# A two-part block on one core: the second 256-token feed-forward block takes the seven-product form, the first one is written out as single jobs, and keys x values and numerators go in eleven chunks of three heads

## The chip, the core and the metric

One Trainium2 chip, one of its cores. The metric is the device time of one execution in microseconds (us). The kernel before was run three times apart from its profile: 374.29, 374.99 and 375.0 us, median 374.99. One more execution was profiled: 374.21 us, in which the program's own span is 372.4 us.

## What is computed

```python
sa, ca, ga, sb, cb, gb = split(silu(c) @ w_mod)          # six rows of 576
h = layernorm(x) * (1 + ca) + sa                          # x: 2048 x 576
q, k, v = split(h @ wqkv)                                 # 32 heads of 18
phi(t) = concat(softmax(t @ w_phi), softmax(-(t @ w_phi)))   # 36 features a head, q and k
kv, z = phi(k)^T v, sum(phi(k))                           # linear attention, a head at a time
x = x + ga * ((phi(q) kv / (phi(q) z + 1e-6)) @ wo)
h = layernorm(x) * (1 + cb) + sb
x = x + gb * (relu(h @ w1) @ w2)                          # w1: 576 x 4608, w2: 4608 x 576
```

All inputs and the output are bf16.

## The kernel before, in words

**Tiles and stages.** The 2048 tokens are 16 tiles of 128. The kernel has three stages.

1. *Setup and the walk over the tokens.* The weights of k and q are folded with w_phi on TensorE (jobs `FK`, `FQ`), three rows of constants are added to the folded weights so that the layernorm's mean and shift come out of the same product (jobs `KR`, `VR`, `QR`), and for each tile the products K, V and Q are made (`proj`, ten matmuls of 116 rows x 288 columns each). ScalarE takes the exponentials, VectorE the sums, GpSimd the ratios. `kv` (line 331) adds each tile's phi(k)^T v into two PSUM banks.
2. *Attention and feed-forward, in eight blocks of two tiles.* For a block, `num_mm` (line 401) makes the numerators and denominators, `num_o` divides, a DMA transposes, `wo_mm`/`project` (lines 418, 958, 965) or seven products (lines 984, 989) make the output projection; then the second layernorm; then layer 1 (h @ w1, relu) and layer 2 (the product with w2, in seven products of 18 matmuls of 288 columns, line 890).
3. *The end*: the last half product, its sum and the stores.

**Layer 1 has two forms.** Blocks 0 and 1 use `l1` (line 744): 324 matmuls of 64 rows x 128 columns of weights, each with 256 tokens moving (324 is 18 pairs of column blocks x 9 chunks of 64 features x 2; two matmuls with different halves of the 128 rows run beside each other). Blocks 2 to 7 use `l1_seven` (lines 793 and 810): 7 products of half size in place of 8 (Strassen's scheme), in 512 matmuls with 128 tokens moving and 36 with 256. The seven products need sums of the weights (`w1_sum`, line 486, 512 or 2048 elements a partition at a time, in place, once) from additional copies of w1 parts (`w1_more`), and sums of the features of each block (`t_feat`, line 868, four a block). The constant `BS = 2` is the number of blocks in the old form.

**Keys x values in nine chunks.** phi(k) of a tile is 1152 columns wide (32 heads x 36). Before, these are cut into nine pieces of 128, which don't fall on the heads' borders: a piece touches four or five heads, so `kv` has nine matmuls a tile with 76 columns (five of them) or 95 (four), and a mask takes out what belongs to other heads. `num_mm` uses the same nine pieces, one split at a bank's border: ten matmuls a tile with 76 (four), 95 (four) and 38 columns (two).

**What sets the order of the work.** `tc.manual_schedule()`: each engine runs its instructions in the order in which the program issues them. For stage 1, and for stage 2 up to the first layernorm of the feed-forward, that order is the string `ORDER`, one word a job (`K7:1` is the K product of tile 7 into PSUM pair 1; `eK7` its exponentials on ScalarE; `sK7` the sums on VectorE; `pM7` a GpSimd job; `LwqT` a load on the SyncE queue). Blocks 0 and 1 are then driven by hooks called between the matmuls (`b0_l1`, `in_l1`, `in_l2`), blocks 2 to 7 by the string `SEVEN` and hooks. All loads, stores, transposes and round trips through DRAM are issued on one queue, SyncE's (SP); one load is on ScalarE's.

**What the steps of the prediction touch.** `spin` (line 238) are matmuls on zeros that fill TensorE's time at the start. `rows_mm` (line 276) makes the K and V constant rows with ten matmuls of 288 columns; the Q row goes through `quarters` (line 373), twenty matmuls of 144 columns with 32 columns of weights, of which four run beside each other. `add_res` (line 426) adds a projection to x and so frees the two PSUM banks that it read; `relu` (lines 752 to 754) has two ScalarE instructions and one on VectorE; `t_part` (line 512) makes sums of w2; `q_sm` (lines 292 and 350) sums a tile of phi(q); `ln2_apply` (line 435) applies the second layernorm.

Of the kernel before, what the change touches and what calls it, by code (L numbers as in the profile page):

```python
# [7 lines left out]
P = 128  # L8
# [24 lines left out]
KVC = [((P * c) // E36, (P * c + P - 1) // E36) for c in range(9)]  # L33
# [3 lines left out]
for _c, (_a, _b) in enumerate(KVC):  # L37
    _k = 0 if _c < 5 else 1
    KVO.append((_k, _o[_k]))
    _o[_k] += (_b - _a + 1) * VW  # L40
# [8 lines left out]
Lt2 pM1 V1:0 m2:2 eK3 FQ0:3 Lx6 vE0 V2:1 Lwga vE1 rK2 Lx10 m2c FQrd0 pA2 FQ1:3 xa4 sp4 Lt4 bn7 vE2 T4:2 Tc4 K4:0 FQra1  # L49
eK4 FQ2:2 xp6 bn6 sa6 FQrd2 sK3 Lt3 bn11 K5:1 pM2 kv0 kv1 QR:2 eK5 V3:0 kv2 QRh sp6 QRe QRd T6:2 rK3 sK4 pA3 vE3 rp  # L50
Tc6 pM3 K7:1 rK4 K6:2 pM4 pA4 eK7 eK6 Lwgb ga:0 gac V4:1 bn9 kv3 sK5 rK5 bn8 pA5 w2b0 sa8 V5:2 vE4 bn12 sp8 T8:0 xa8
pM5 vE5 Tc8 Q0:1 eQ0 gb:2 xp14 kv4 kv5 sK6 bn10 Q1:0 gbc sa10 sK7 gaw gar wl1 rK6 K8:1 qs0 wl3 bn15 eQ1 eK8 K9:2 eK9
sp10 xp10 Lwo Q2:0 pA6 sK8 pM6 eQ2 V6:1 rK8 bn13 vE6 sK9 bn14 qp0 rK7 Q3:2 pA8 T10:0 Tc10 pA7 eQ3 qs1 pM7 kv6 K10:1
eK10 rK9 K11:0 sK10 pM8 V8:2 eK11 sa14 sa12 V7:1 vE8 pM9 rK10 V9:0 vE7 xa12 sp12 pA9 kv7 T12:2 sK11 rK11 kv8 V10:1 vE9
kv9 wl0 pA10 vE10 Tc12 pM10 K12:0 sp14 T14:2 Tc14 gbw eK12 kv10 K13:1 eK13 wo2 K14:2 eK14 qt0 qs2 sK12 sK13 Q4:0 eQ4
rK13 K15:1 w2a1 qp1 V11:2 V12:0 gbr qs3 wo1 pA11 qp2 pM11 vE11 kv11 w2a2 rK12 w2a0 pA12 eK15 vE12 sK15 pM12 qt1 V13:2
kv12 pM13 Lmask sK14 Q5:1 wl4 rK15 eQ5 sq5 Q6:0 pA13 pA15 vE13 sq4 kv13 qt2 V15:2 rK14 vE15 pM15 pA14 V14:1 vE14 eQ6
Q11:2 pM14 qp3 sq6 kv14 kv15 qt3 eQ11 sq11 Q7:1 kz nu1:2 Q8:0 nu0:3 nO1 td2 eQ7 eQ8 sq7 nO0 td0 sq8 ot1:2 td1 Q9:1 oc1
Q10:0 ot0:2 wo0 wo4 eQ9 qi5 wo3 sq9 oc0 eQ10 W1:3 xr1 qi4 W0:1 lb1 Q12:2 xr0 lb0 Q13:0 lr1 eQ12 sq10 qi6 lr0 ap1 eQ13
Q14:1 ht1:2 Q15:3 ap0 wl2 ht0:0 ha eQ14 eQ15 hd w2b1 sq13 sq15 sq14 sq12  # L60
# [16 lines left out]
BS = 2  # L77
# [4 lines left out]
def tile_block(ctx, tc, a, out):  # L82
# [18 lines left out]
    x_sb = small([P, NT, D], BF16, "x_sb")  # L101
# [3 lines left out]
    NEQ, NE, NV, NL = 6, 5, 4, 3  # L105
    TW = 18 * HD
    RTL = 17920
    RT = small([P, RTL + NL * 2 * D], BF16, "RT")
    v_sb = carve(RT, 0, (NV, H * VW))
    E_sb = carve(RT, NV * H * VW, (NE, 2 * D))  # L110
    xT_hi = NE * 2 * D + NV * H * VW
    EQ = carve(RT, xT_hi + 8 * NC * P, (NEQ, 2 * D))
    SLOT = (0, 1, 2, 3, 4, 5, 0, 1, 2, 3, 4, 5, 0, 1, 2, 3)
    EL = carve(RT, RTL, (NL, 2 * D))
    eqd = dram.tile([P, NT, 2 * D], BF16, name="eqd")
    NET = 4
# [28 lines left out]
    kvz = small([P, KVW], BF16, "kvz")
    ga_row = small([P, D], BF16, "ga_row")
# [84 lines left out]
    pool.memset(epsz, 0.5e-6)  # L231
    pool.memset(m98[:], 0.0)
# [40 lines left out]
    def rows_mm(raw, pr):  # L273
        for k in range(2):
            for ck in range(NC):
                pe.matmul(pr[0:NX, k, 0:HD], lhsT=m98[0:R, ck, :], rhs=raw[0:R, ck, k * HD:(k + 1) * HD],
                          start=(ck == 0), stop=(ck == NC - 1))

# [6 lines left out]
    def exps(t, pr, E):  # L285
        for s in range(2):
            act.activation(out=E.rearrange("p (b h s e) -> p b h s e", b=2, s=2, e=DH)[:, :, :, s, :],  # L287
                           in_=pr[:, :, 0:HD].rearrange("p b (h e) -> p b h e", e=DH),
                           func=ACT.Exp, scale=rs[:, t, s:s + 1])

    def sums(E, Rr):
        dve.tensor_reduce(out=Rr, in_=E.rearrange("p (c e) -> p c e", e=DH), axis=AXX, op=ALU.add)

# [33 lines left out]
    def kv(t):  # L327
        E = E_sb[:, t % NE, :]
        for c in range(9):
            k, o, n = kvcols(c)  # L330
            pe.matmul(PS[:, 6 + k, o:o + n], lhsT=E[:, c * P:(c + 1) * P],  # L331
                      rhs=v_sb[:, (t + 1) % NV, KVC[c][0] * VW:KVC[c][0] * VW + n],
                      start=(t == 0 and o == 0), stop=(t == NT - 1), skip_group_check=True)
# [4 lines left out]

    def eq(u):
        return EQ[:, SLOT[u], :] if u < QF else EL[:, u % NL, :]  # L340

    def q_out(u):
        sp.dma_start(eqd[:, u, :], EQ[:, SLOT[u], :])

    def q_in(u):
        sp.dma_start(EL[:, u % NL, :], eqd[:, u, :])

    def q_sm(u):
        sums(eq(u), Rq[:, u % 2, :])
        dve.reciprocal(out=rq[:, u % 2, :], in_=hs(Rq[:, u % 2, :], 1))  # L350

    def q_pool(u):
        pool.tensor_tensor(out=ratq[:, u % 2, :], in0=hs(Rq[:, u % 2, :], 0), in1=rq[:, u % 2, :], op=ALU.mult)
        minus(pool, eq(u), ratq[:, u % 2, :])

    def eslot(u):
        return u % NET if u < 8 else u % 2

    def q_turn(u):
        sp.dma_start_transpose(ET[:, eslot(u)], eq(u).rearrange("p (c f) -> p c f", f=P))  # L360
# [21 lines left out]
    def row_r(k):  # L382
        sp.dma_start((ga_row, gb_row)[k][:], gatd[k:k + 1].rearrange("a g f -> a (g f)").to_broadcast([P, D]))

    def num_mm(t, pr):
        seen = set()
        parts = []
        for c in range(9):
# [5 lines left out]
        for i, (c, h0, h1) in enumerate(parts):  # L394
# [6 lines left out]
            pe.matmul(pr[:, k, b:b + n], lhsT=ET[:, eslot(t), c, :], rhs=kvz[:, o:o + n],  # L401
# [60 lines left out]
    w21 = x_sb[:, 8:16, :].rearrange("p a b -> p (a b)")[:, 0:4096]  # L462
# [29 lines left out]
    TF = carve(RE.bitcast(FP16), 2 * 9 * P, (4, 4, P))  # L492
# [32 lines left out]

    def rows_h(pr, k):
        c = slice(k * HD, (k + 1) * HD)
        act.activation(out=tmpr[X0:NX, c], in_=pr[X0:NX, k, 0:HD], func=ACT.Copy)

    def rows_d(pr, dst, k):  # L530

        c = slice(k * HD, (k + 1) * HD)
        dve.scalar_tensor_tensor(out=dst[X0:NX, 4, c], in0=tmpr[X0:NX, c], scalar=mk[X0:NX, :],
                                 in1=pr[X0:NX, k, 0:HD], op0=ALU.mult, op1=ALU.add)
# [20 lines left out]
    def scale():  # L555
        dve.tensor_scalar(out=ca1[0:R, :], in0=PS[0:R, 7, 0:NC], scalar1=1.0, scalar2=None, op0=ALU.add)
        dve.tensor_scalar(out=m98[0:R, :, X0:X0 + 3], in0=ca1[0:R, :].unsqueeze(2).to_broadcast([R, NC, 3]), scalar1=-1.0,
                          scalar2=None, op0=ALU.mult)

    def x_scale(t, eng):  # L560
# [6 lines left out]
        for ck in range(NC):  # L567
# [64 lines left out]

    def t_cols(t, pr):
        for j in range(2):
            pe.transpose(bf(pr[:, 0, :])[:, j * P:(j + 1) * P], sc[:, (t + j) % 4, :], ident[:, 0:P])

    def rows_copy(t, pr):
        act.activation(out=xt_rows(t, 2), in_=bf(pr[:, 0, :])[X0:NX, 0:2 * P], func=ACT.Copy)  # L638

    def stats_a(t):  # L640
        act.activation(out=lnv[:, t:t + 2], in_=mv[:, 0, t:t + 2, 1], func=ACT.Ln, bias=eps_t[:], scale=1.0)
        act.activation(out=rs[:, t:t + 2, 0], in_=lnv[:, t:t + 2], func=ACT.Exp, scale=-0.5)
        act.activation(out=sc[:, t % 4:t % 4 + 2, X0 + 3], in_=lnv[:, t:t + 2], func=ACT.Exp, scale=0.5)

    def stats_p(t):
        c = sc[:, t % 4:t % 4 + 2, :]
        pool.tensor_copy(c[:, :, X0:X0 + 2], mv[:, 0, t:t + 2, 0:1].to_broadcast([P, 2, 2]))
        pool.tensor_tensor(out=c[:, :, X0 + 2], in0=mv[:, 0, t:t + 2, 0], in1=c[:, :, X0], op=ALU.subtract)
        pool.tensor_scalar(out=rs[:, t:t + 2, 1], in0=rs[:, t:t + 2, 0], scalar1=-1.0, scalar2=None, op0=ALU.mult)

    def k_scale(t):
        pool.tensor_scalar(out=Ak[:, t % 4, :], in0=hs(rk[:, t % 4, :], 0), scalar1=rs[:, t, 0:1], scalar2=None, op0=ALU.mult)

    def k_minus(t):
        Rr, r = Rk[:, t % 4, :], rk[:, t % 4, :]
# [646 lines left out]
```

## Time and profile before

| | |
|---|---|
| median of three runs | 374.99 us (374.29 to 375.0) |
| the profiled execution, its own time | 374.21 us |
| its span | 372.4 us |
| TensorE (PE) busy | 365.9 us of the span |
| VectorE (DVE) busy | 291.5 us |
| ScalarE (ACT) busy | 225.3 us |
| GpSimd (POOL) busy | 147.3 us |
| granted TensorE clock | 1.0 |
| PE waits that the trace names, all | 2.5 us, all before 18 us |

How it is read: an engine's busy share over the span says little by itself, since stages have different limits; what counts is the chain of work that ended last, which the profile follows back from the last instruction, and the order on each engine's queue. The duration of one matmul in a group's row is from issue to its end, with much of it overlapped by the next: the spacing of the starts is what a matmul costs TensorE.

### The profile page before, as it was taken

The numbers are of one execution on the slowest core, as the hardware profiler recorded it, in microseconds if no ns is written. First come the engines' busy times: TensorE is split into PE (matmuls) and PEld (weight loads), VectorE is DVE, ScalarE is ACT, GpSimd is POOL, SyncE is SP. The second block draws the span as 40 slices with busy tenths as digits, with TensorE's granted clock in tenths as the row PEclk, the third lists the DMA queues.
The fourth block names the chain that finished last, engine by engine and source line by source line (L and its number), as shares of the span: only waits on it lengthen the run. The fifth ranks groups of instructions, "written<-read, shape, count | busy, mean of one in ns | idle before, by whom it ended". The sixth has DMA issues, their size and how long they took to land.

```text
span 372.4 us, 14350 instructions
## 1 busy us (share of the span) xinstructions
PE 365.9 (98%) x6236; PEld 312.4 (84%) x6237; DVE 291.5 (78%) x540; ACT 225.3 (60%) x507; POOL 147.3 (40%) x215
## 2 busy tenths in 40 slices
PE   7999999999999999999999999999999999999996
PEld 3778788888888788889988987998799889879975
DVE  3999997679979789987897689679777857755742
ACT  2598998588632535608853874578277628835720
POOL 2167999940302567380056007402720260043023
PEclk9999999999999999999999999999999999999999
DMA  8994799787976437572164248413422304101001
GB/s 298 414 371 158 273 409 327 205 235 297 277 170 133 121 83 160 150 136 60 36 113 116 35 35 128 102 38 69 99 63 20 84 18 53 36 0 35 4 2 33
DMA packets 58880, 50.26 MB, mean 135 GB/s; under 512 B 46912, under 2 KB 51136, under 8 KB 58048
## 3 DMA queue, kind: packets, MB, share of 16 engines
q1 hardware_dynamic: 58672, 49.18, 48.9%
q8 instruction: 49, 0.80, 0.9%
q10 hardware_dynamic: 144, 0.16, 0.2%
q14 instruction: 15, 0.12, 0.1%
HBM read 32.27 MB, written 5.90 MB: 103 GB/s over the span
## 4 chain that ended last, share of the span: by engine, by line
PE 93%; DMA 4%; ACT 1%; SPq 0%; issue 0%; DVE 0%
PE PS L890 33%; PE PS L810 23%; PE PS L282 15%; PE PS L744 10%; PE PS L793 3%; DMA R<-in_wqT_dram 3%; PE PS L984 2%; PE PS L401 2%; DMA R<-in_wsc_dram 2%; PE PS L958 2%; PE PS L331 2%; PE PS L418 1%; PE PS L930 1%; ACT R L570 1%; PE PS L989 0%; PE PS L373 0%
## 5 line engine op out<-in xcount | busy, mean ns | idle before, releaser
L890 PEld LDWEIGHTS <-RH 128*128 128x128 f16 x846 | 81.5, 98 | 21.0 <-issue 0.4
L878 POOL TENSOR_TENSOR yt<-yt,gb_row 128x288 f32<-128x288 f32 x23 | 27.3, 1186 | 169.8 <-DVE yt L877 169.8
L810 PEld LDWEIGHTS <-R 64*128 64x128 bf16 (+1 forms) x1824 | 76.1, 94 | 0.7 <-issue 0.2
L890 PE MATMUL PS<-R,RH 128*128 128x288 bf16 (+1 forms) x558 | 74.5, 286 | 0.0
L810 PE MATMUL PS<-h,R 64*128 64x128 bf16 x1056 | 69.3, 216 | 0.0
L840 ACT ACTIVATE RH<-PS 128x512 f16<-128x512 f32 x96 | 50.9, 604 | 9.2 <-PE PS L810 9.1
L810 PE MATMUL PS<-RE,R 64*128 64x128 f16 x768 | 48.2, 216 | 0.0
L287 ACT ACTIVATE RT<-PS,rs 128x576 bf16<-128x576 f32 x64 | 42.9, 746 | 3.6 <-PE PS L282 3.4
L890 PE MATMUL PS<-RT,RH 128*128 128x288 f16 x288 | 38.6, 286 | 0.0
L744 PE MATMUL PS<-h,R 64*128 64x256 bf16 (+1 forms) x684 | 36.3, 264 | 0.0
L744 PEld LDWEIGHTS <-R 64*128 64x128 bf16 x684 | 31.6, 94 | 4.0 <-issue 0.2
L1047 ACT ACTIVATE h<-h,mod 128x256 bf16<-128x256 bf16 x63 | 32.8, 588 | 2.3 <-DMA h<-xn 2.3
L282 PE MATMUL PS<-RH,R 116*128 116x288 bf16 x240 | 32.5, 286 | 0.1
L810 PE MATMUL PS<-h,early 64*128 64x128 bf16 x384 | 32.0, 216 | 0.0
L282 PE MATMUL PS<-RH,RT 116*128 116x288 bf16 x240 | 31.5, 286 | 0.0
L243 DVE BATCH_NORM_STATS2 st<-x_sb 128x6 f32<-128x288 bf16 x64 | 25.8, 446 | 6.4 <-DMA x_sb<-in_xk_dram 6.3
L282 PEld LDWEIGHTS <-RT 116*128 116x128 bf16 x240 | 22.9, 98 | 5.5
L282 PEld LDWEIGHTS <-R 116*128 116x128 bf16 x240 | 22.6, 98 | 5.9 <-ACT R L638 0.4
L877 DVE TENSOR_TENSOR yt<-PS,RS 128x288 f32<-128x288 f32 x23 | 10.4, 452 | 20.6 <-PE PS L890 14.1
L810 PEld LDWEIGHTS <-w 64*128 64x128 f16 (+1 forms) x480 | 26.5, 94 | 0.0
L879 POOL TENSOR_TENSOR x_sb<-yt,x_sb 128x288 bf16<-128x288 f32 x30 | 24.9, 832 | 2.6 <-DVE yt L875 0.8
L810 PE MATMUL PS<-RE,w 64*128 64x128 f16 x384 | 25.9, 216 | 0.0
(179 smaller groups left out, 744.0 us busy)
## 6 DMA issues: line engine op xcount, KB each, us to landing
R<-in_w_dram SPq DMA_DIRECT2D x4, 1152.0 KB
eqd<-RT SPq DMA_DIRECT2D x12, 288.0 KB, 4.1
RT<-eqd SPq DMA_DIRECT2D x12, 288.0 KB, 3.0
R<-in_w2b_dram SPq DMA_DIRECT2D x2, 1296.0 KB, 6.9
R<-in_w2a_dram SPq DMA_DIRECT2D x3, 864.0 KB
out_dram<-x_sb SPq DMA_DIRECT2D x15, 144.0 KB, 1.8
x_sb<-in_xk_dram SPq DMA_DIRECT2D x10, 144.0 KB
RT<-in_xT_dram SPq DMA_DIRECT2D x2, 640.0 KB, 6.3
```

The lines of the kernel that those rows point to most:

```text
L243: dve.bn_stats(out=s[:, hf, :], in_=x_sb[:, t % 6 if n else t, hf * HD:(hf + 1) * HD])
L282: pe.matmul(pr[:, k, 0:HD], lhsT=xt(t, ck), rhs=w[0:R, ck, k * HD:(k + 1) * HD], start=(ck == 0), stop=(ck == NC - 1))
L287: act.activation(out=E.rearrange("p (b h s e) -> p b h s e", b=2, s=2, e=DH)[:, :, :, s, :], in_=pr[:, :, 0:HD].rearrange("p b (h e) -> p ...
L744: pe.matmul(PS[:, 2 * u + hf, n * 256 + o:n * 256 + o + w], lhsT=w1_lhs(hf, c, j, h), rhs=hb[b0:b0 + 64, c, o:o + w], start=(n == 0 and c ...
L793: pe.matmul(PS[:, bank_at[n], j * 256:j * 256 + 256], lhsT=w1_lhs(hi, c, j, hi), rhs=hb[64 * hi:64 * hi + 64, c, :], start=(j == 0 and c = ...
L810: pe.matmul(PS[:, bank_at[BK[n] + str(g)], i * P:(i + 1) * P], lhsT=w[r, (4 * c + i) * P:(4 * c + i + 1) * P], rhs=x, start=(n in ("M1", " ...
L840: act.activation(out=o, in_=v[{"k11": "Y", "k12": "Z", "k21": "X", "k22": "W"}[n]], func=ACT.Relu)
L877: dve.tensor_tensor(out=y, in0=PS[:, bank, 0:HD], in1=SS[:, s, :], op=ALU.add)
L878: pool.tensor_tensor(out=y, in0=y, in1=gb_row[:, c], op=ALU.mult)
L879: eng.tensor_tensor(out=xs(t)[:, c], in0=y, in1=xs(t)[:, c], op=ALU.add)
L890: pe.matmul(PS[:, bank, 0:HD], lhsT=am[:, j, :], rhs=bm[:, j, :], start=first and j == 0, stop=(j % 9 == 8), skip_group_check=True)
L1047: act.activation(out=o, in_=o, func=ACT.Identity, scale=mod(1, c), bias=mod(0, c))
```

## The change

1. `BS` is 1: block 1 goes through `l1_seven` with the hooks of the later blocks. All weight sums and feature sums that it needs are made one block earlier, all weight sums on VectorE in pieces of 2048 elements (before, eight pieces of 512 were on GpSimd).
2. Block 0 is no more a loop with hooks. Its layer 1 is nine jobs `lm0` to `lm8`, its relus `lu`, its layer 2 fourteen half products `pa0` to `pa13`, its attention, sums of w2, layernorm and stores are jobs too, all words in `ORDER`.
3. `KVC` has eleven chunks of three heads (108 of the 128 rows are the chunk's own, the rest belong to the next and are masked). `kv` has eleven matmuls a tile, ten with 57 columns and one with 38; `num_mm` twelve, nine with 57, two with 38, one with 19. The tiles of phi(q) that go through DRAM come back with eleven pieces of 128 columns a row, and are transposed in eleven pieces (before nine).
4. The K and V constant rows go through `quarters` too: twenty matmuls of 144 columns in place of ten of 288; V's rows then travel by four small DMAs, as Q's do.
5. Statistics, ratios and reciprocals of K are made for two tiles at a time, the rows of statistics for four tiles from tile 4 on; the second layernorm of tiles 2 and 3 goes to ScalarE (`ln2_act`); five more spins stand near the start (27 in place of 22).
6. `ORDER` is new throughout. GpSimd zeroes four more regions at the start.

```diff
-KVC = [((P * c) // E36, (P * c + P - 1) // E36) for c in range(9)]
+NKC = 11
+KVC = [(3 * c, min(3 * c + 2, H - 1)) for c in range(NKC)]
+KVS = [3 * E36 * c for c in range(NKC)]
...
-Lbdw Z11 LwkT FK Z1 fra1 Lx0 Lcc sx bn0 sd frd2 Lwsc frd0 bn1 sa0 frr sc ca Lwsh frd4 Lx2 Lid bn3 sh fra3 sp0 T0:1 shc
-Lt0 KR:2 KRh0 Lwv Lx4 xd0 bn2 KRh1 mk KRd0 KRd1 Tc0 sa2 Ka0:0 VR:1 bn4 VRh0 Kb0 VRd0 sp2 VRh1 Lt1 xd2 Ka1:2 Kb1 VRd1
-T2:1 eKa0 sK0 LwqT FQ3:3 Tc2 K2:0 FQra3 bn5 Lwsb eKa1 sK1 K3:3 rK0 eK2 sa4 FQ4:2 FQrd4 pM0 V0:1 sK2 Lwcb rK1 pA1 pA0
...
+Lbdw Z11 LwkT Lx0 Lcc Lwsc bn0 sx Z3 sd FK bn1 sa0 sp0 fra2 fra0 Lwsh fra4 Z2 Lx2 Z1 frd3 rp frd1 Lid mk Lt0 Lwv sc
+Lx4 Lt1 LwqT ca sh frr bn3 xv0 T0:1 shc KR:3 xu0 Tc0 Ka0:0 bn2 KRh Lx6 KRd1 sa2 KRd2 KRd0 VR:2 VRh KRd3 bn4 Kb0 Ka1:1
+Kb1 Lt2 bn5 sp2 T2:3 VRe eKa0 sK0 eKa1 sK1 FQ2:0 bn6 FQra2 FQ1:2 xp2 Tc2 K3:1 VRd FQra1 K2:3 FQ3:0 eK3 Lwcb eK2 FQ4:2
...
+ht0:3 ha ou3 hd ou2 lm0:2 td2 eQ15 te2 te1 lm4:3 tb0 tc0 lm1:1 qi4 qi6 eQ14 sq14 lu0 wf3:0 wm6 wf2:2 lu4 wr2 wt0 wt2
+xR3 qs4 xR2 lb2 gbw sq12 lm5:3 lu5 qt5 lm2:0 lm6:2 lu1 qp4 lm3:1 lu2 qs6 tb2 lm7:3 lb3 lu6 tb1 lr2 aP2 lu3 lu7 tc1
+lm8:0 lu8 lr3 lv1 pa0 pa1 qt4 nu4:0 wt5 qp6 sq15 sq13 nO4 lv0 pa2 lv2 wm4 px gbr hT2 pa3 tc2 aP3 hT3 nu5:0 py qi7 wt7
+pc0 pa4 pa5 wt6 pc1 pf0 pa6 pa7 hS1 nO5 pa8 pc2 pa9 pa10 ou4 hS0 pf1 ou5 hS2 qt6 pa11 pa12 qs7 pa13 tf1 tf0 pf2 po1
+wm5 tf2 tf3 qi9 pf3 qp7 qt7 wt4 qi8 po0
...
-BS = 2
+BS = 1
...
-        for c in range(9):
+        for c in range(NKC):
             k, o, n = kvcols(c)
-            pe.matmul(PS[:, 6 + k, o:o + n], lhsT=E[:, c * P:(c + 1) * P],
-                      rhs=v_sb[:, (t + 1) % NV, KVC[c][0] * VW:KVC[c][0] * VW + n],
+            pe.matmul(PS[:, 6 + k, o:o + n], lhsT=E[:, KVS[c]:KVS[c] + P],
+                      rhs=v_sb[:, t % NV, KVC[c][0] * VW:KVC[c][0] * VW + n],
                       start=(t == 0 and o == 0), stop=(t == NT - 1), skip_group_check=True)
...
     def q_in(u):
-        sp.dma_start(EL[:, u % NL, :], eqd[:, u, :])
+        src = eqd[:, u, 0:P]
+        sp.dma_start(el(u).rearrange("p (c f) -> p c f", f=P),
+                     bass.AP(src.tensor, src.offset, [list(src.ap[0]), [3 * E36, NKC], [1, P]]))
...
-    for w in "KV":
-        JOBS[w + "R"] = lambda w=w: rows_mm(ROWS[w], at[w + "R", None])
...
+    JOBS["KR"] = lambda: quarters(at["KR", None], lambda ck: m98[0:R, ck, 28:60], wk)
...
+    for i, w in enumerate("QV"):
+        JOBS[w + "R"] = lambda w=w: quarters(at[w + "R", None], lambda ck: m98[0:R, ck, 0:32], ROWS[w])
...
+    def ln2_act(t):
+        act.activation(out=nrs[:, t % 2, 0:1], in_=rs2[:, t, 0:1], func=ACT.Copy, scale=-1.0)
+        act.activation(out=nrs[:, t % 2, 1:2], in_=mv[:, 1, t, 0:1], func=ACT.Copy, scale=nrs[:, t % 2, 0:1])
+        o = xn[:, t % 2, :].rearrange("p (c d f) -> p c d f", d=2, f=64)
+        for d in range(2):
+            act.activation(out=o[:, :, d, :], in_=xs(t).rearrange("p (c f) -> p c f", f=64), func=ACT.Identity,
+                           scale=rs2[:, t, 0:1], bias=nrs[:, t % 2, 1:2])
...
+    JOBS.update({
+        "lm": lambda u: l1_mm(u, at["lm", u]), "lu": lambda u: relu(u, at["lm", u]), "lv": add_u2,
+        "pa": prod2, "pc": keep, "pf": lambda i: fin(*F2[i]), "po": store,
...
+        "ou": o_turn, "wf": lambda i: wo_full(i, at["wf", i]), "xR": lambda i: add_res(i, at["wf", i]),
+        "wr": lambda i: (wo_rest(i, at["wf", i]), wo_rest(i + 1, at["wf", i + 1])),
+        "hS": lambda k: h_scale(1, k), "tf": lambda k: t_feat(1, k), "hT": h_turn, "aP": ln2_act,
+        "tb": lambda k: t_part(1, k), "tc": lambda k: t_part(2, k), "te": lambda k: t_part(3, k),
...
+        "ws": lambda i: w1_sum(i // 2, i % 2, pool), "wt": lambda i: w1_sum(i // 2, i % 2),
+        "wm": lambda i: w1_more(i // 2, i % 2),
+    })
...
-    for b in range(NB):
-        if b < BS:
-            l1(b, (2, 0, 2, 0, 1, 3, 1, 3, 2) if b == 0 else (2, 1, 0, 3, 2, 1, 0, 3, 2), in_l1(b) if b else b0_l1)
-        else:
-            l1_seven(b, in_seven(b))
+    held.append(7 + NL)
+    project(4, WO)
+    for b in range(1, NB):
+        l1_seven(b, in_seven(b))
         l2(b, in_l2(b))
```

More of the change, by code (lines that the diff above doesn't have):

```diff
@@ L387, in num_mm @@
         parts = []
-        for c in range(9):
+        for c in range(NKC):
             h0, h1 = KVC[c]
@@ L566, in x_scale @@
             return
-        for ck in range(NC):
+        for ck in cks:
             v, f = xt(t, ck, 2), ca1[0:R, ck:ck + 1]
@@ L631, in kv_job, with many @@
             kv_eps()
+    def many(t):
+        return 2 if t < 4 else 4
     def t_cols(t, pr):
[L634 removed]
+        for j in range(many(t)):
             pe.transpose(bf(pr[:, 0, :])[:, j * P:(j + 1) * P], sc[:, (t + j) % 4, :], ident[:, 0:P])
     def rows_copy(t, pr):
[L638 removed]
+        act.activation(out=xt_rows(t, many(t)), in_=bf(pr[:, 0, :])[X0:NX, 0:many(t) * P], func=ACT.Copy)
     def stats_a(t):
[L641 removed]
@@ L932, in l2, with prod2, keep, store @@
         sp.dma_start(outf[rows, HD:D], xs(t)[:, HD:D])
+    LO, HI = range(9), range(9, NK)
+    P2 = ((X, A11, B11, LO, 1), (X, A11, B11, HI, 0), (Y, A12, B21, LO, 1), (Y, A12, B21, HI, 0), (X, U2, T2, LO, 0),
+          (X, U2, T2, HI, 0), (Z, A11, T1, LO, 1), (X, U3, T3, LO, 0), (X, U3, T3, HI, 0), (Z, A11, T1, HI, 0),
+          (X, A22, T4, LO, 0), (X, A22, T4, HI, 0), (Z, A12, B22, LO, 0), (Z, A12, B22, HI, 0))
+    def prod2(i):
+        bank, am, bm, js, first = P2[i]
+        for j in js:
+            pe.matmul(PS[:, bank, 0:HD], lhsT=am[:, j, :], rhs=bm[:, j, :], start=(first == 1 and j == 0), stop=(j % 9 == 8),
+                      skip_group_check=True)
+    def keep(i):
+        act.activation(out=SS[:, i, :], in_=PS[:, X, 0:HD], func=ACT.Copy)
+    F2 = ((0, 0, Y, 0), (1, 1, Z, 2), (1, 0, X, None), (0, 1, Z, 1))
+    def store(i):
+        sp.dma_start(outf[i * P:(i + 1) * P, :], xs(i))
     NB = NT // 2
```

366 lines of the change are left out of this document (161 added, 205 removed).

## The prediction, made before the changed kernel ran

> **What bounds the kernel now.** I read the page's busy shares first (TensorE 98%), then the chain of work that ended last, then the waits of TensorE, then busy times by stretch. The chain, in order of time (columns: start, length, what; xN is the number of matmuls):
>
> ```profile
> 2.11 6.05 DMA R<-in_wsc_dram
> 8.18 9.69 DMA R<-in_wqT_dram
> 17.91 0.45 PE PS L267 x6
> ...
> 29.84 0.69 PE PS L331 x18
> 30.54 0.43 PE PS L373 x20
> 30.96 1.33 PE PS L282 x10
> 32.29 0.35 PE PS L331 x9
> ...
> 76.85 0.38 PE PS L401 x10
> ...
> 130.25 17.68 PE PS L744 x324
> 147.94 2.31 PE PS L890 x18
> ...
> 201.22 0.95 PE PS L810 x33
> ...
> 217.48 2.31 PE PS L890 x18
> ...
> 366.62 2.26 PE PS L930 x36
> ```
>
> Up to 17.9 us the chain is the loading of weights; wqT is the last load that TensorE needs. From there to 368.9 it is TensorE almost without a break. All of TensorE's waits that the trace names:
>
> ```profile
> PE PS L238 <- POOL eps_t L230: 1.3, 1, 1.3
> PE PS L259 <- DMA R<-in_wsc_dram: 0.5, 1, 0.5
> PE PS L259 <- DVE ca L556: 0.4, 1, 0.4
> PE PS L267 <- DMA R<-in_wqT_dram: 0.3, 1, 0.3
> ```
>
> So after 17.9 us there is nothing to win by removing waits: a microsecond comes from fewer or cheaper matmuls, and every new wait is paid in full. Before 17.9 us fewer matmuls are worth nothing as long as wqT lands when it does. The sums below are made against the profiled execution, 374.21 us with a span of 372.4; the median of the runs, 374.99, lies 0.8 above it.
>
> **Block 1's layer 1: -1.4 us.** Its 324 matmuls take 17.68 us (130.25 to 147.94). A block in seven products takes 16.26 (201.22 to 217.48). The other blocks in that form lie at 16.3, so block 1 saves 17.68 - 16.3 = 1.4. Layer 2 is the same 126 matmuls in both forms.
>
> **Eleven chunks: -1.3 us, wide bounds.** `kv` and `num_mm` are on the chain with 0.35 and 0.38 us a tile, 16 tiles each. What a narrow matmul costs is the distance of starts; the trace's starts give these medians: at L331 34 ns for 76 columns and 42 for 95; at L401 27 for 38, 37 for 76, 45 for 95. In both lines 19 columns less are worth 8 ns, so 57 columns come to 26 and 29; as 38 columns already cost 27, I take 27 and 29. `kv`: before 5 x 34 + 4 x 42 = 338 ns, after 10 x 27 + 27 = 297. `num_mm`: before 4 x 37 + 4 x 45 + 2 x 27 = 382; after 9 x 29 + 2 x 27 + 25 (one column costs 25: 50 matmuls of L259 take 1.24 us) = 340. Together -83 ns x 16 = -1.3. Bounds: all 57-column ones at 27 gives -1.6; if 57 columns cost what 76 do (34 and 37), `kv` has 367 and `num_mm` 412, together +59 ns x 16 = +0.9. I stay with -1.3, as both lines show the slope.
>
> [...]
>
> **The head: 0.** Two rows jobs go from 1.23 us (ten matmuls of 123 ns, as L282 x10) to 0.43 (the row L373 x20): -1.6 on TensorE. But the list of SyncE's issues has the same twelve loads up to wqT in the same order, so wqT lands near 17.86 again. TensorE's list after `sh` (12.0 us) is T0, KR, Ka0, VR, Kb0, Ka1, Kb1, T2: 0.2 + 0.43 + 0.98 + 0.43 + 0.25 + 0.98 + 0.25 + 0.1 = 3.6, and the rows must come through ScalarE and VectorE to Kb0 (about 0.8): done near 16.5, 1.4 before wqT. The three more spins before `FK`, at 0.4 us each (11 took 4.38), push `FK` from 5.8 to at most 7.0 and `sc` from 8.2 to at most 8.9; the 1.4 covers that. If wqT came 1.1 earlier, 1.1 would be won. GpSimd's additional zeroing (by its 512-element row, 0.53 us, some 4 us) ends near 6.5, its next work was at 10.1. V's rows by four DMAs hold SyncE's queue for the wcb and wsb loads behind them; in before both have landed by 21.8, and their use is at 23.4: if that cover went, `m2` would wait, up to 0.5.
>
> **The walk over the tokens (18 to 77 us): 0 beside the above.** Work to the end of `kv`, by the durations of the rows, in us before and after: TensorE 57 and 55, VectorE 52 and 53, ScalarE 50 and 45, GpSimd 52 and 50. The pairs in `k_r` and the rows for four tiles pay for the rest; all helpers stay below TensorE. Bound +0.7 for waits in between.
>
> **Block 0 (90 to 130 us): +1.0.** This is where the new form's price is paid. Busy times in that stretch before (columns: stretch, its length, then busy us and instructions of PE, PEld, DVE, ACT, POOL):
>
> ```profile
> 90.20:130.30 40.10, 40.10 (x571) 33.17 (x572) 35.43 (x62) 18.88 (x46) 10.75 (x11) 1.00 0.76 192
> ```
>
> VectorE has 35.4 of 40.1. After, it has in the same stretch: six weight sums of 2048 (1.29, 1.58, 2 x 1.58, 2 x 1.61 = 9.2, by the L486 rows) in place of two (2.6): +6.6; four `t_feat`, +2.7 (2 x 0.42, 2 x 0.93); one more `q_sm`, +1.7; and less: two attentions that now stand earlier, 2 x (0.35 + 0.76) = -2.2; `ln2_apply` of two tiles, now on ScalarE, -2.0 (which has room: 18.9 of 40); three sums of wo, -1.6. Sum 40.6. TensorE has 40.1 less two numerators that also stand earlier (0.9): 39.2. VectorE is 1.4 over, and TensorE needs it for each bank that it reuses. The place can be followed in the order. From `lm0` to `lm2` TensorE has lm0 (72 x 28 ns) 2.0, lm4, lm1 and lm5 2.0 each, two projections 2.3: 10.3. lm2 needs pair 0, which xR3 frees. Ahead of xR3 on VectorE's queue stand td2, te2, te1, tb0, tc0 (5 x 0.97 in sequence), two relus 0.7, wt0 and wt2 2.9, itself 0.7 = 9.1, from about 1.3 after lm0's start, with 0.5 of hand-overs: 10.9, so 0.5 late. lm6 needs xR2: qs4 1.7 and xR2 0.7 later, while TensorE has lm2, 2.0: 0.4 more. At block 1's start add_res stands behind wt4 (1.6): 0.1 to 0.6. I take 1.0. Bounds: 0 (VectorE is early) and 6.1 (the second rival).
>
> GpSimd loses its weight sums (a GpSimd of 10.7 in 40: worth nothing). The reload of phi(q) with 1408 pieces of 256 bytes, and transposes of 11 pieces in place of 9, lengthen a path that had 15 us and more from the reload's landing to the numerators in the later blocks: 0. w21 and w22 now load before block 0; if w21's first part came later than 98 us, wt0 and all behind it would move with it.
>
> **Sum**: -1.4 - 1.3 + 0 + 0 + 1.0 = -1.7. From 374.21 that is 372.5 (span 370.7), from the median 373.3; I forecast 372.9, halfway.
>
> **Rivals.**
> 1. *No wait in block 0*: ScalarE's layernorm and the early sums let VectorE keep up. For it: its excess, 1.4, is small beside what could be done before 90 us. Against: it was busy 9.2 of the ten microseconds from 90 already. Sum -2.7: 371.9.
> 2. *VectorE's own waits stay: slower.* Before, VectorE stood idle 4.7 us of the 40.1, mainly in front of add_res (2.7 behind L965), in front of relus (0.9 behind ScalarE) and of `fin` (0.6). If W of these remain although the queue is full, the stage takes 40.6 + W, and TensorE loses 1.4 + W. At W = 3.4 that is 4.8: 374.6 - 2.7 + 4.8 = 376.7. It decides from W = 2.1 on (1.4 + 2.1 - 2.7 = +0.8). Against: these waits stood where VectorE had caught up, and a queue that is behind has none. For: relus and add_res still follow matmuls.
> 3. *Narrow matmuls have a price of their own*: the load of 128 columns of weights, not the columns that move, spaces them, and the 64 additional ones (four a tile) cost as 76 columns. -1.4 + 0.9 + 1.0 = +0.5: 375.1. Against: 27 ns for 38 columns with weights of their own.
> 4. *wqT lands 1.1 earlier*, and the shorter rows show: 371.8. Against: the loads ahead of it have not changed.
>
> [...]
>
> **Chances**: forecast 0.46, first rival 0.19, second 0.14, third 0.11, fourth 0.10. 0.2% (0.75 us) is about what a measurement of this kernel can tell from no change. Faster: 0.41 of the forecast's 0.46, the first and the fourth rival: 0.70. Same: 0.05 and most of the third: 0.14. Slower: the second and a part of the third: 0.16. The range leaves out the second rival's far end and the best corner (no wait and the head's 1.1 together): 370.9 to 375.7.
>
> **What will show it.** The chain: L825 and L808 for block 1, in 16.3 us; a tile's `kv` at 0.31 us and `num_mm` at 0.34 (0.37 and 0.41 for the third rival); wqT still on the chain near 17.9, with over 1 us of TensorE's wait in front of `FQ`. TensorE's waits on VectorE in layer 1 of block 0 (L771) near 0.9 us, and before L808 or L825 of block 1 up to 0.6; none for the first rival, over 3.5 for the second. VectorE nearly full from 90 to 131. I would be wrong if the walk over the tokens got waits of its own, or if a load came late in block 0.

## The result, and the profile after

The changed kernel takes 376.54 us in the median (374.24 to 378.99, 20 executions), the kernel before 374.6 (373.58 to 375.44, 20 executions, the three of the start among them): ratio 1.0052, 95% interval 1.0033 to 1.0071. It is **slower by 0.5%**; the forecast was 372.9. The profiled execution took 377.21 us, 0.7 above the median.

The head of the page (its span, and the clock granted to TensorE in 40 slices):

```profile
span 375.4 us, 14948 instructions
...
PEclk9998999999999999999999999999999999999999
```

The clock isn't 1.0 throughout any more: slice 4 (28 to 37 us) has 0.8. The chain of work that ended last, with the lines that answer to those of before (start, length, what):

```profile
22.00 7.02 DMA RE<-in_wsb_dram
29.06 1.40 PE PS L273 x50
...
30.47 0.33 PE PS L343 x11
...
78.51 0.33 PE PS L435 x12
...
95.40 5.89 DMA oT<-o_sb
101.34 2.13 PE PS L989 x16
...
134.13 0.95 PE PS L825 x33
...
143.15 1.35 issue
144.50 7.64 PE PS L825 x267
152.14 2.31 PE PS L905 x18
...
205.20 0.95 PE PS L825 x33
...
221.46 2.31 PE PS L905 x18
...
370.32 2.26 PE PS L942 x36
```

Two transfers now stand on it far behind the head: the load of `wsb`, and the transposes of o for the projection of tiles 2 and 3, which is made inside block 0's layer 1. Block 1's layer 1 goes from 134.13 to 152.14, 18.0 us in place of the 16.26 of a later block (205.20 to 221.46), with a hole of 1.35 in it that nothing in the profile explains ("issue"). TensorE's waits (what waited, for what: us in total, times, longest):

```profile
PE PS L989 <- DMA oT<-o_sb: 1.6, 1, 1.6
PE PS L825 <- issue: 1.3, 1, 1.3
PE PS L252 <- POOL eps_t L240: 1.3, 1, 1.3
PE PS L273 <- DMA RE<-in_wsb_dram: 0.8, 1, 0.8
PE PS L290 <- DVE RH L553: 0.7, 1, 0.7
...
```

No line names VectorE in block 0. The stretch behind m2 by twos of microseconds (busy us and instructions of PE, PEld, DVE, ACT, POOL; then TensorE's granted clock, DMA share, GB/s):

```profile
28.00:30.00 2.00, 1.24 (x57) 1.05 (x46) 1.97 (x7) 0.83 (x3) 1.92 (x5) 1.00 0.98 405
30.00:32.00 2.00, 2.00 (x40) 1.64 (x38) 1.80 (x6) 1.05 (x5) 1.50 (x2) 0.78 1.03 419
32.00:34.00 2.00, 2.00 (x11) 1.19 (x9) 1.10 (x4) 0.73 (x2) 0.41 (x2) 0.50 0.87 221
34.00:36.00 2.00, 2.00 (x16) 1.52 (x15) 1.32 (x1) 1.45 (x4) 0.00 (x0) 0.87 0.68 255
```

TensorE is called full from 30 us on, but between 32 and 34 it starts 9 products of line 290 (the row counts the 11 that were under way), and 16 of them from 24 to 26: it runs at half its clock.

**Where the time went.** I read the starts of TensorE's landmarks off both timelines. "Expected" is before, changed by what the edit moves or cheapens.

| stretch of TensorE | before | expected | after | over |
|---|---|---|---|---|
| to FQ's first matmul (wqT) | 17.91 | 17.91 | 18.06 | 0.15 |
| FQ to the first `kv` | 11.77 | 10.9 | 12.27 | 1.4 |
| `kv` to the first numerator | 47.01 | 46.3 | 48.01 | 1.7 |
| numerator to block 1's layer 2 | 71.18 | 70.7 | 73.73 | 3.0 |
| the rest to the last matmul | 220.78 | 220.3 | 220.27 | 0 |

Second row: less one product that now stands later (1.23) and the two matmuls of T4 (0.1), plus QR (0.43), which stood behind the first `kv` before. Third: QR -0.43, `kv` -0.40, T4 +0.1. Fourth: that product +1.23, layer 1 of both blocks 36.04 to 34.6, numerators -0.28. The expected column is 2.6 under before, and the holes are 6.3: 3.7 more, which is what the last matmul is later by (the span is 3.0 longer, as the end behind that matmul is 0.7 shorter). Of the holes: 0.15 in front of FQ, 0.6 in FQ, 0.8 m2's wait for wsb, 1.7 in the walk (1.5 of it that its 320 projection matmuls take 40.95 us, and 39.43 before), 1.2 in block 0's layer 1 with the wait for oT in it (19.55 us against 18.34 in `wm_at_51_spin` below, which has no such wait), 1.75 in block 1's.

### The profile page after: what moved, and what is told of

Read it like the earlier page. It is cut to its first block, busy times and chain, and to the rows that moved or that the text cites. A ratio compares the mean times of both kernels' runs of the same rounds, so it can differ in the third digit from the quotient of the medians.

```text
span 375.4 us, 14948 instructions
## 1 busy us (share of the span) xinstructions
PE 365.9 (97%) x6549; PEld 311.7 (83%) x6550; DVE 294.0 (78%) x538; ACT 233.6 (62%) x499; POOL 136.9 (36%) x191
## 4 chain that ended last, share of the span: by engine, by line
PE 92%; DMA 3%; ACT 2%; DVE 1%; issue 1%; SPq 0%; POOL 0%; POOLq 0%
PE PS L905 28%; PE PS L825 27%; PE PS L290 13%; PE PS L954 4%; PE PS L808 4%; PE PS L771 3%; PE PS L252 2%; DMA RE<-in_wsb_dram 2%; PE PS L1014 2%; PE PS L989 2%; DMA oT<-o_sb 2%; ACT RT L296 1%; PE PS L435 1%; PE PS L343 1%; PE PS L273 1%
## 5 line engine op out<-in xcount | busy, mean ns | idle before, releaser
L825 PEld LDWEIGHTS <-R 64*128 64x128 bf16 (+1 forms) x2128 | 88.7, 94 | 2.3 <-issue 1.7
L905 PEld LDWEIGHTS <-RH 128*128 128x128 f16 x738 | 71.0, 98 | 18.2
L825 PE MATMUL PS<-h,R 64*128 64x128 bf16 x1232 | 81.0, 216 | 0.0
L855 ACT ACTIVATE RH<-PS 128x512 f16<-128x512 f32 x112 | 59.4, 603 | 12.0 <-PE PS L825 11.8
L905 PE MATMUL PS<-R,RH 128*128 128x288 bf16 (+1 forms) x486 | 65.0, 286 | 0.0
L825 PE MATMUL PS<-RE,R 64*128 64x128 f16 x896 | 56.3, 216 | 1.3 <-issue 1.3
L825 PE MATMUL PS<-h,early 64*128 64x128 bf16 x448 | 37.5, 216 | 0.0
L825 PE MATMUL PS<-RE,x_sb 64*128 64x128 f16 x448 | 29.2, 216 | 0.0
L825 PEld LDWEIGHTS <-early 64*128 64x128 bf16 x448 | 28.3, 94 | 0.1
L825 PEld LDWEIGHTS <-x_sb 64*128 64x128 f16 x448 | 25.0, 94 | 0.2 <-issue 0.2
```

Source lines behind the costliest of these rows:

```text
L825: pe.matmul(PS[:, bank_at[BK[n] + str(g)], i * P:(i + 1) * P], lhsT=w[r, (4 * c + i) * P:(4 * c + i + 1) * P], rhs=x, start=(n in ("M1", " ...
L855: act.activation(out=o, in_=v[{"k11": "Y", "k12": "Z", "k21": "X", "k22": "W"}[n]], func=ACT.Relu)
L905: pe.matmul(PS[:, bank, 0:HD], lhsT=am[:, j, :], rhs=bm[:, j, :], start=first and j == 0, stop=(j % 9 == 8), skip_group_check=True)
```

## The experiments

Two theories stood after this. **Loads**: holes where a load lands late cost the time. **Clock**: the holes are small, but they let the granted clock fall to half for a few microseconds (a *fall* below), and that costs it. For the second: of the 20 executions above, the three with a mean clock of 1.000 take 374.24 to 374.85, the six with 0.990 or 0.991 take 376.92 to 378.99. The edits are to words of `ORDER`, one a line. `Z3` is three spins; `Lwsb` loads wsb; `m2` is the fifty one-column products that read wcb and wsb, `m2c` their copy; `QR` the twenty narrow products of the Q row; `wm0`, `wm2`, `wm5` are loads of 512 KB of weights, `wt0` to `wt2` sums of weights on VectorE that read such loads; `ou` transposes o, `wf` projects it, `xR` is add_res.

### The changed kernel again

No edit.

> The changed kernel, nothing edited. Clock theory: the loss is mostly the lower granted clock near 31 to 35 us, which follows a sparse stretch of TensorE (waits, fifty one-column products) from 28 to 31 us; executions with a mean clock of 1.0 should then take 374.2 to 374.9, those with 0.995 some 1.8 more, and the median come out near 376.5 again. Load theory: the loss is three holes, 0.8 us before m2, 1.6 before the projection of tiles 2 and 3, 1.35 in block 1's layer 1 under 'issue'; they should be there again in this profile, whatever its clock. If the 1.35 is an accident of one execution it is gone here.

376.76 us (10 executions), ratio 1.0055 (1.0031 to 1.0078): the loss is there again. The holes are read from the profiles below.

### One hole at a time

`spin_m2`, `wsb_early`, `oT_early`:

```diff
 bn9
+Z3
 m2:2
```

> Three spins of 512 columns (0.21 us each) ahead of m2, into its 0.8 us wait; no load moves. Clock theory: TensorE is not idle there any more, the clock stays at 1.0 from 30 to 36 us, the span is 1.5 to 1.8 shorter than the unedited kernel's, 374.8. Load theory: the wait for wsb only gets a different occupant, nothing is won: 376.5.

375.39 (12 executions), ratio 1.0033 (1.001 to 1.0056): 1.4 less than the unedited kernel on the same chip. 11 of 12 executions have a mean clock of 0.999 or more, unedited 3 of 10. No load moved, so the **clock** theory holds in the head. What is left is in block 0. The profile is of the one execution in twelve that has a fall (377.4 us); TensorE waits for oT 3.0 us in it, and the clock falls behind that hole:

```profile
PE PS L989 <- DMA oT<-o_sb: 3.0, 1, 3.0
```

```profile
98.00:100.00 2.00, 0.49 (x10) 0.21 (x4) 1.35 (x3) 0.07 (x1) 0.00 (x0) 1.00 0.82 32
100.00:102.00 2.00, 0.48 (x3) 0.31 (x4) 1.10 (x1) 0.00 (x0) 0.00 (x0) 0.84 0.87 176
102.00:104.00 2.00, 2.00 (x10) 1.29 (x9) 1.35 (x2) 0.00 (x0) 0.00 (x0) 0.50 1.35 219
```

In the same profile block 1's layer 1 has no hole: 135.89 to 152.24, 16.35 us.

```diff
+Lwsb
 VRd
...
+FQ0:3
 V1:1
-FQ0:3
...
-Lwsb
```

> wsb's load is issued ahead of V's four row DMAs in place of behind them, and FQ0 stands ahead of V1 on TensorE. wsb should land near 23 in place of 29.0 us; the rows land near 23.1, so that V1 may wait 0.3. Load theory alone: m2's 0.8 goes, 0.3 comes: 376.0. Clock theory: with the wait the low clock goes too: 374.2.

377.21 (6 executions), ratio 1.0084 (1.0055 to 1.0114). A miss: m2's wait is gone and the clock stays at 1.0 in the head, but FQ waits 1.0 for ScalarE, a `kv` 1.3 for VectorE, and the projection 2.3 for oT, with a fall behind it. The new order can be blamed for the first of these at most: the wait of `kv` is in the profile of `fill_holes` too, where nothing in the walk was moved but for the three spins, and that for oT in the unedited kernel.

```diff
-wm2
-wm0
...
 ou2
+wm2
+wm0
```

> The loads wm2 and wm0 (two parts of 512 KB) are issued behind the two transposes of o in place of ahead of them. At 400 GB/s they take 2.6 us, so the first transpose should land near 98.5 in place of 101.3 and the projection's 1.6 us wait go: 374.9 by the load theory. The clock theory says nothing on this one: its drop stays, 374.9 too. Rival: the transposes are held by the phi(q) stores and w2b's last part, which stay ahead, and nothing is won (376.5); or wt0 comes late for lack of wm0 and gives it back.

380.7 (6 executions), ratio 1.0158 (1.0131 to 1.0184): much worse, by the second rival. The transposes have no wait any more; the wait is elsewhere:

```profile
PE PS L771 <- DVE x_sb L460: 4.6, 1, 4.6
```

```profile
96.91 6.58 DMA x_sb<-in_w_dram
...
103.52 1.24 DVE x_sb L520
```

wm0 takes 6.6 us from its issue to landing; the weight sum that reads it (`wt0`, line 520) stands ahead of `add_res` (460) on VectorE, and TensorE needs the banks that add_res frees. So moving the two loads by a few microseconds serves one and delays the other: in the profile after, the projection could start at 99.7 (101.34 less its wait), wt0 at about 101, and sums of w2 ahead of both read w2b's last part.

### Is it the idle time or the landing?

`fill_holes` is `spin_m2` with twelve spins more, in the projection's own banks:

```diff
+        "Zf": lambda i: spin(i, 0),
...
+Zf12
 wf3:0
```

> No load moves. Spins of 512 columns (0.21 us each) are put into the two holes: three ahead of m2, twelve (2.6 us) ahead of the projection of tiles 2 and 3, into its own PSUM banks. Clock theory: the waits stay, but TensorE is busy in them and the clock stays at 1.0; against the kernel with the three spins alone (375.4) the 2 us that the matmuls behind the transposes' wait lost are won: 374.0, and the spread of the executions shrinks. Load theory: what costs is the landing, and spins change nothing (375.4), or they delay the projection where the transposes land early (376).

375.94 (11 executions), ratio 1.0046 (1.0026 to 1.0065). All executions have a clock of 0.999 or more, the profile shows 1.00 from 98 to 104 us, and nothing is won over 375.39. Two things limit what this shows. Eleven of the twelve executions of `spin_m2` had no fall either, so there was little for these spins to save in the median. And in this profile the first transpose lands at 101.6 us while the projection starts behind the spins at 102.1, so they were some 0.5 too many. What it leaves is that both kernels are slower than before at a clock of 1.0: in block 0 the low clock is *not* what costs in the median, and the **load** theory remains, to be tried by moving loads.

The other three of that set moved the sums wt0 and wt2 behind both add_res (`oT_early_wt_late` starts from `oT_early`; the next has `Z3` as well; the last is `spin_m2` with the sums moved, so its loads stay where they were):

```diff
-wt0
-wt2
 xR3
 qs4
 xR2
+wt0
+wt2
```

> As the kernel with wm2 and wm0 behind the transposes of o, and also the two weight sums that read them (wt0, wt2) behind both add_res on VectorE. If the 4.6 us wait there was wt0 standing in front of add_res, it goes now; the projection has no wait, no clock drop follows: 376.8 - 2 to 3 = 374.3. If VectorE is full in block 0 (its price of +1.0 in the prediction), the 2.5 us of sums come out as waits at L771 or L808 instead: 375.5.

> The same with three spins ahead of m2. Both drops of the clock should be gone: 1.4 less than without the spins, 372.9 by the clock theory with loads in time; no difference to the one without spins if the clock in the head is not what costs.

> wm2 and wm0 stay ahead of the transposes; only the sums wt0 and wt2 go behind both add_res, and three spins stand ahead of m2. The wait of the projection for the transposes (3.0) stays with the clock drop behind it: 375.4 as with the spins alone, if the transposes' landing is the cause; 374 if it was VectorE's sums that held the path.

380.94, 379.36 and 379.85 (6 each), ratios 1.0158 (1.0117 to 1.0199), 1.0138 (1.011 to 1.0166) and 1.0125 (1.0099 to 1.0152). Three misses. In the second of them the chain goes over the reload of phi(q) (97.99 for 7.58 us), which the sum in front of the second add_res reads, and TensorE waits 3.4 for add_res and 1.2 for a relu; in the third, where no load moved, VectorE's relu is 2.2 late, oT 2.4, and the clock falls in the head in spite of the three spins (0.5 from 30.59 us for 3.41, behind a wait of 0.5 for wsb). Moved behind add_res, the two sums (1.2 us each) delay what follows; in their old place they stood where VectorE waited for the projection anyway (2.2 us in front of add_res in `spin_m2`).

### Take the loads out of the crowd

SyncE's queue issues a DMA at 51.60 us and the next at 65.83, since that one waits for other engines; the places that wm2 and wm0 write are free by then.

```diff
 w2a1
+wm2
+wm0
...
-wm2
...
-wm0
```

> The loads wm2 and wm0 are issued behind w2a1, near 51.6 us, in place of near 92: SyncE's queue then waits until 65.8 for other work, and the DMA engines fall to half a share at 64 to 66. Three spins stand ahead of m2. Load theory: 1 MB less stands ahead of the transposes of o and of the loads behind them; the transposes land by 98.5, the sums wt0 and wt2 find their data, the wait of 1.6 to 3.2 and the clock drop behind it go: 375.4 - 2.5 = 372.9. Clock theory: the same by way of the clock, at least 1.0 of it. Rival: VectorE is full in block 0 as the prediction priced it, and up to 1.0 comes out as TensorE's waits at L771 or L808: 373.9.

373.76 (12 executions), ratio 0.9994 (0.998 to 1.0007): 1.6 less than `spin_m2`, and nothing else moved (the two were timed on different chips, on which the kernel before took 374.24 and 374.27). The transposes land in time, and of TensorE's waits none is in block 0 any more:

```profile
PE PS L252 <- POOL eps_t L240: 1.3, 1, 1.3
PE PS L290 <- DVE RH L553: 0.7, 1, 0.7
PE PS L825 <- issue: 0.5, 1, 0.5
PE PS L281 <- DMA R<-in_wqT_dram: 0.5, 1, 0.5
PE PS L290 <- ACT RT L296: 0.3, 2, 0.2
```

VectorE is as full in that stretch as the prediction feared; first this kernel, then the kernel before:

```profile
88.00:131.00 43.00, 42.91 (x592) 36.78 (x592) 41.63 (x70) 26.80 (x63) 8.56 (x10) 1.00 0.83 176
```

```profile
88.00:131.00 43.00, 43.00 (x612) 35.64 (x611) 37.99 (x70) 20.89 (x51) 11.45 (x12) 1.00 0.77 202
```

41.6 of 43 us, and this profile names no wait of TensorE for it in block 0 (three later ones have one of 0.2).

Next, three variants of it: also `wt1` moved; that without `Z3`; that with `Z3` and `wm5` moved.

```diff
-wt1
...
 rK12
+wt1
```

> The same, and the weight sum wt1 stands behind rK12 on VectorE in place of ahead of sK13: its load landed at 61 us while VectorE was there at 59.5, and in two profiles the products keys x values waited 1.3 us for what stood behind it. If that wait is there in most executions, 0.5 to 1.3 less than the run without this edit: 372.0; if only in some, 0.3 less and a smaller spread.

> As the one before, without the three spins ahead of m2. Clock theory: the drop at 31 to 35 us is back in about half of the executions, 1.4 more in the median than with the spins, and the clock of those executions is 0.995. If the loads moved also make m2's wait go, no difference.

```diff
 wm4
+wm5
...
-wm5
```

> As the kernel with wm at 51, wt1 moved and the spins, and the load wm5 (512 KB) is issued right behind wm4 near 114 us in place of near 132, where it stands ahead of TensorE's instruction fetch of 136.85 us. If the hole of 0.3 to 1.35 us in block 1's layer 1 comes from a fetch that stands behind data, no hole of over 0.2 is in this profile and the median is up to 0.5 lower; if the hole has another cause, it is still seen in some profiles.

373.57, 374.54 and 373.73 (12 each), ratios 0.9989 (0.9972 to 1.0006), 1.0002 (0.9982 to 1.0021), 0.999 (0.9977 to 1.0003). wt1's place is worth 0.2, no more than the measurement tells. Without the spins 7 of 12 executions fall to a clock of 0.995; their median is 374.86, that of the other five 372.75. So an execution with the fall, and the wait ahead of it, takes some 2.1 us more, and the executions without it reach the forecast (372.9). In this profile, which has the fall, the trace puts m2's wait down to VectorE's statistics of another tile:

```profile
PE PS L273 <- DVE st L257: 0.7, 1, 0.7
```

That is a wrong name. The trace records the landing of a load in sixteen parts; the last part of wsb comes at 28.63 us, and m2 starts at 28.68. In the profile after it is 29.02 and 29.06. So m2 waits for wsb again, and moving wm2 and wm0 has not changed that. wm5's place decides nothing: a hole of 0.3 remains in block 1.

### What sets off the lower clock

All four start from `wm_at_51_wt1`, without spins unless said: QR ahead of V2; m2 in two halves, wcb's ahead of V2, wsb's in its old place; one spin ahead of m2; m2 and its copy behind K4.

```diff
+QR:1
 V2:0
-QR:1
```

> On the kernel with wm at 51 and wt1 moved (374.5, of which executions at clock 1.0 took 372.75 and those at 0.995 took 374.9): QR's twenty narrow products (0.43 us) stand ahead of the product V2 in place of behind it, no spins. The sparse stretch ahead of kv0 is shorter by 0.43 us. If the clock falls by how long TensorE is sparse, fewer executions fall: 373.5. If the wait for wsb alone decides it: 374.5 with the same share of executions at 0.995.

```diff
-        "m2": lambda: mods([wsb, wcb], at["m2", None]), "m2c": lambda: mod2_e(at["m2", None]),
+        "m2a": lambda: mods([wcb], at["m2a", None][:, :, NC:]), "m2b": lambda: mods([wsb], at["m2a", None]),
+        "m2c": lambda: mod2_e(at["m2a", None]),
...
+m2a:2
 V2:0
...
-m2:2
+m2b
```

> m2's half that reads wcb (which lands at 26 us) stands ahead of V2, the half that reads wsb (27.5 to 29 us) behind QR; no spins. Two sparse pieces of 0.6 and 1.1 us with a dense product between them in place of one of 1.7, and half of m2 done while wsb is still on its way: up to 0.6 of the wait goes. Clock theory: no drop, 372.7. Load theory for the wait: at 0.995 as often as before, but 0.4 less: 374.1.

```diff
+Z1
 m2:2
```

> One spin (0.21 us) ahead of m2 in place of three or none. If a short activity in the stretch is enough to hold the clock: 373.1, no execution at 0.995. If the length of the sparse stretch decides: a share of executions at 0.995 between those without spins (7 of 12) and with three (none).

```diff
-m2:2
-m2c
...
 K4:0
+m2:2
+m2c
```

> m2 stands behind K4, some 1.7 us later, so that wsb has landed in every execution; no spins. The wait for wsb is gone: 0.8 less in the executions that had it, and the clock holds if the wait was part of the stretch that drops it: 372.7. Rival: K4 needs tile 4's rows, which ScalarE copies late, and a wait for that takes the place of m2's: 373.5 to 374.5.

| kernel | executions with a clock of 0.999 or more | median, us | ratio (interval) |
|---|---|---|---|
| no spin (`wm_at_51_wt1`) | 5 of 12 | 374.54 | 1.0002 (0.9982 to 1.0021) |
| QR first | 8 of 12 | 374.49 | 0.9995 (0.9977 to 1.0012) |
| m2 behind K4 | 10 of 12 | 374.96 | 1.0017 (0.9993 to 1.0041) |
| one spin | 11 of 12 | 374.08 | 0.9976 (0.9957 to 0.9995) |
| three spins (`wm_at_51_wt1_spin`) | 12 of 12 | 373.57 | 0.9989 (0.9972 to 1.0006) |
| m2 split | 12 of 12 | **373.45** | **0.997 (0.9955 to 0.9985)** |

(QR first, m2 behind K4, one spin and m2 split were timed on a chip where the kernel before took 374.73; on the chip of the other two it took 374.24. The kernel without a spin was not timed on the first of these chips, so that its falls would be as many there is not shown.) Less of the sparse stretch, fewer falls: with QR out of it the wait for wsb is left (1.0 us, put down to VectorE again: wsb's last part comes at 28.86, m2 starts at 28.90) and falls go from 7 to 4 of 12; one spin of 0.21 us leaves one. With a dozen executions each, the order of the rows is plain at its ends, not between neighbours.

Chance enters in part by wsb's last part. It comes by 27.5 us in four profiles (`spin_m2`, `oT_early`, `fill_holes`, `m2_one_spin`), and m2 doesn't wait in them; in most others it comes at 28.3 to 29.3, up to 1.5 us behind the part before it. Among the profiles with a late one, m2 whole in its place and no spins, the clock falls in four and stays in one (`oT_early_wt_late`, with a wait of 1.0). So the profile with one spin can't show that one spin holds the clock through a wait. That of m2 split does: wsb comes at 29.00, half of m2 is done by then, the wait is 0.3 and the clock stays.

m2 behind K4 pays for its place, if by other waits than its rival named: in its profile TensorE waits 0.7 for VectorE ahead of tile 4's rows and 0.6 for m2's copy.

**m2 split beats both kernels**, by 0.3% under before; as the best of fifteen edited kernels it may owe a part of that to the choice. Its profile in the stretch of the fall:

```profile
28.00:30.00 2.00, 1.74 (x59) 1.31 (x58) 1.76 (x6) 0.94 (x5) 1.92 (x5) 1.00 1.01 413
30.00:32.00 2.00, 2.00 (x24) 1.63 (x21) 1.93 (x7) 1.19 (x6) 1.36 (x2) 1.00 1.03 424
32.00:34.00 2.00, 2.00 (x19) 1.59 (x17) 1.96 (x5) 2.00 (x4) 0.41 (x2) 1.00 0.93 221
```

## Why the prediction was wrong, point by point

- **Block 1's layer 1, -1.4: right**, where there is no hole: 16.35 us against the forecast 16.3. The hole (1.35 here, 0 to 1.2 in all in the profiles of the other edits) was in no term, and it is the largest single loss.
- **Eleven chunks, -1.3: right.** By TensorE's starts a tile's `kv` goes from 354 ns (5.66 us by 16) to 329, its numerators from 397 (2.38 by 6) to 350. Together -72 ns, 16 times -1.15; the numerators gave a little more than forecast, `kv` 25 ns in place of 41. The third rival (a narrow matmul's own price, 367 and 412 ns) falls with it.
- **The head, 0: wrong by 1.4.** wqT came as forecast (FQ starts at 18.06), but "if that cover went, `m2` would wait, up to 0.5" was what happened, and 0.8. The step took the landing of wsb from before (under 21.8). V's four row DMAs wait for VectorE and hold SyncE's queue until 21.5 in the order, so wsb is issued at 22.0 and lands at 29.0. The margin ahead of FQ was mis-sized too: `FK` starts at 7.23 (at most 7.0 forecast), `sc` at 9.4 (8.9), the rows wait 0.7 for VectorE, and the work ahead of FQ ends near 17.8 in place of 16.5. So the sign "over 1 us of TensorE's wait in front of `FQ`" is not in this profile; the others have a wait of 0.5 to 1.5 there.
- **The walk, 0: wrong by 1.7**, not by a helper that is too slow, but by the clock: behind m2's wait it was 0.5 for 3.41 us, and with spins in that wait 11 of 12 executions kept 0.999 or more (`spin_m2`), unedited 3 of 10. The prediction had every wait at its own length; this one cost 0.8, and 1.5 more in the products behind it.
- **Block 0, +1.0 by VectorE: wrong term, similar size.** VectorE is full (41.6 of 43) and TensorE didn't wait for it; the first rival was right there. The price came from the loads: the sentence "if w21's first part came later than 98 us, wt0 and all behind it would move with it" named a load (w21 is wm0's place), though for the sum behind it and not for the transposes, and I gave it no number. From 85 us to the transposes at 95.4 SyncE asks for 576 + 1296 + 3 x 304 + 2 x 512 KB, 3.9 MB; at the 332 GB/s that the trace shows in that window, this is 11.7 us, so the transposes behind it couldn't land before 97 at the best. The first landed at 101.3. The bytes explain that part alone; what held the transposes for the other 4 us is not shown (see the last section).
- **The second rival's 376.7 is near the time by chance**: its mechanism (VectorE's old waits stay, and TensorE waits over 3.5 us for it) is not in the changed kernel's profile, which names no wait for VectorE in block 0.

So the step that failed is the one that priced the moved loads at nothing: 0 for wsb in the head, 0 for its wait in the walk, and no term for the transposes behind the loads in block 0. The gains were there, 2.6 by the table; late transfers on one queue (wsb, oT) cost 2.0, the walk with its clock 1.7, FQ and what stands ahead of it 0.75, block 1's hole 1.75. The runs show the cause of the first two by taking it away (`wm_at_51_spin`, `spin_m2`, `m2_split`); that of the hole in block 1 and of FQ's 0.6 stays open. With two loads 40 us earlier, wt1 moved and m2 in halves the kernel stands at 0.997 of before; the forecast 372.9 was 0.9965 of the profiled 374.21.

The range ended at 375.7, under the 376.54: its ends held the bounds of single terms, and no term for a load behind others.

## What to carry to other kernels

When work moves a block earlier, add up the bytes that the queue is asked for ahead of each transfer with a due time, at the rate that the trace shows there; that gives the earliest time, not the likely one (here 97 us, and the transposes landed at 101.3). A queue with a hole 40 us before is the place for a load that waits for nothing (1.6 us less in `wm_at_51_spin` than in `spin_m2`). A wait in a stretch of narrow matmuls isn't priced by its length alone: look at the granted clock in the microseconds behind it (here 0.8 us of wait, then 0.5 for 3.41 us, which cost 1.5 more). An engine that is 97% busy (VectorE, 41.6 of 43 us) need not hold the path, if its order puts the work where it would have waited.

## What the runs showed of the hardware

- **The clock fell behind a gap of 0.8 us.** In the profile after, that gap of TensorE lies between twenty products of 32 columns of weights and fifty of one column; then the trace's record of the granted clock has 0.5 from 31.11 to 34.52 us (3.41 us; windows of 0.78, 0.50 and 0.87). In all profiles with a fall inside the program its length is 3.41 us or a multiple (6.8 in `again`, behind its wait of 3.2 for oT), and so is the time at 1.0 ahead of it: 23.89 us is 7 times 3.41 (after, `wm_at_51_wt1`), 27.31 is 8 times (`qr_first`), 95.57 is 28 times (`spin_m2`). The record starts 4.0 to 7.2 us into the span in these profiles. What sets these times no run shows. Waits of 0.7 us (`wm_at_51_wt1`), 0.8 (after) and 1.0 (`qr_first`) in front of m2 had a fall behind them; one of 1.0 in `oT_early_wt_late` had none (30 projection matmuls took 3.68 us from 30.51, as in `spin_m2` from 30.66).
- **A hole of 1.35 us behind a fetch of instructions.** The trace has instructions as packets of 16,384 bytes on a DMA queue of their own (q8). That they are TensorE's is read from their number: 51 for its 13,099 matmuls and weight loads after, 49 for 12,473 before, 257 and 255 a packet. In the profile after, one goes out at 136.85 us, the next at 142.00 for 0.88; TensorE stops at 143.15 and goes on at 144.50. The packets of the DMA engines in the window 141.95 to 142.9 us, that queue:

```profile
q8 instruction: 1, 0.02, 5.8%
```

  Measured back from the start of block 1's layer 2, that fetch begins 9.9 to 10.45 us ahead in the five profiles with the longest holes behind it (starts 0.75 to 1.6 us apart), and 10.5 to 11.05 ahead in the nine without one behind that fetch; three with small holes (0.4 to 0.5) lie in both ranges. That a late fetch makes the hole is read from these times, not tried by an edit of its own; moving wm5 didn't settle it (a hole of 0.3 remained), and why the fetch comes late stays open.
- **DMA engines that are busy and move little.** In `spin_m2` the window 98 to 100 us has a DMA share of 0.82 at 32 GB/s, while the transposes of o are under way (the first is asked for at 93.9 us and lands at 101.5); packets of 256 bytes, which take 18 ns in the median, last up to 4.5 us there, up to 2.9 in the profile after and up to 0.8 in `wm_at_51_spin`. What they wait for the trace doesn't say.
